# Turning the queries and keys of batches 1 to 3 with transposing transfers of 16-bit halves through DRAM in the place of TensorE

## Chip, cores and metric

One core of a Trainium2 chip runs the whole program. The metric is device time in microseconds (us), from one launch to its end; three runs of the kernel before gave a median of 1028.63 us (1025.24 to 1028.85). Lower is better.

## The reference, cut to what matters

Attention in which a query sees only the keys that chose the same one of 16 centroids, and then a feed-forward block with a squared ReLU:

```python
batch, n_heads, seq, head_dim = (4, 8, 768, 64)
n_clusters = 16
q_assign = np.argmax(np.einsum('bhsd,hcd->bhsc', q_n, c_n), axis=-1)
k_assign = np.argmax(np.einsum('bhsd,hcd->bhsc', k_n, c_n), axis=-1)
mask = q_assign[:, :, :, None] == k_assign[:, :, None, :]
scores = scale * np.matmul(q, k.transpose(0, 1, 3, 2))
scores = np.where(mask, scores, -1000000000.0)
attn = np.exp(scores - max); attn = attn / (sum + 1e-09)
attn_out = np.matmul(attn, v)
# (B, H, S, D) -> x of (3072, 512); w_in (512, 2048), w_out (2048, 512)
h = x @ w_in
out = (np.maximum(h, 0.0) ** 2) @ w_out
```

`q_n`, `k_n` and `c_n` are the rows divided by their norms. Queries, keys, values and centroids are float32; the weights come as 64-bit floats and are rounded in the kernel.

## The kernel before

**Pairs and units.** The 4 batches of 8 heads are worked on as 16 *pairs*: two heads of one batch, whose 64 features lie side by side on 128 partitions. Pairs 0 to 3 are batch 0, pairs 4 to 15 are batches 1 to 3. A pair has 768 queries in two halves of 384 and 768 keys in six chunks of 128. A *unit* is one half of the queries against two chunks of the keys, so a pair has six units. Batch 0 goes first with the first halves of all its pairs (units 0 to 11), then with the second halves (units 12 to 23); after that each pair of batches 1 to 3 takes six units in a row (24 to 95). The loop at L665 goes through the units, with two more rounds, since the product with v (`times_v`) of a unit comes two units after its scores.

**One unit of pairs 4 to 15.** `scores` (L368) issues eight matmuls into two PSUM tiles `sc`. ScalarE takes the exponentials in place (L395, two instructions), and VectorE multiplies by the mask (L399, four), by which the two PSUM tiles come free for the next unit: there are only two. GpSimd sums the exponentials (L409, L411). `times_v` adds eight matmuls. `finish` (L432), some units behind a half's end, sums on TensorE, takes the reciprocal on VectorE (L449) and sends a few rows to `seen` in DRAM (L455). Between these, `fill_steps` puts matmuls of the feed-forward block of batch 0 on TensorE (`ffn`, L469 and L482), in shares that are worked out ahead from a count of columns.

**Preparing the next pair.** For its scores a pair needs queries and keys with the features on the partitions: `qkT`, twelve blocks of 128x128 float32. They are loaded as rows (`load_qk`, four transfers of 192 KB on SP's queue; the pool `loads` has four buffers under the tag `qk`), and `turn` (L244) transposes them on TensorE, four blocks into one bank of PSUM, which ScalarE copies to SBUF (L253), three times for a pair. `logits` (L261) multiplies `qkT` by the centroids, `route` (L274) finds each row's centroid, and `spread` (L331) sends the choices through DRAM (`far`, L340) to all partitions (`qid`, L341), where L399 compares them. `prep` (L346) gives these steps as a list, which goes into `ahead` at the first unit of the pair before; each round of the loop takes up to three entries from `ahead` (L705 to L708), and an entry `None` is an empty turn. For pairs 5 to 15 the list is spaced out at L672, so that the three turns come in the first unit, `logits` in the second, `route` in the third and `spread` in the fourth.

**Order.** Each engine runs its instructions in the order that the framework's scheduler gave it, by the program's order and by priorities: the matmuls of `scores`, `times_v` and `logits` are pulled together (`together`, L86). So the place of an instruction can differ from that in the program, but it is fixed when the kernel is built. SP's queue too is worked through in order, and a transfer that waits holds up those behind it. `qkT` of pairs 0, 1 and 4 to 15 has two buffers (`qktp`).

**Behind the units.** After unit 95 the feed-forward block of the other batches runs in `ffn_pair`, with no part in the change. The weights are loaded and rounded during units 0 to 23 (`load_weights`, L137).

Of the kernel before, what the change touches and what calls it, by code (L numbers as in the profile page):

```python
# [8 lines left out]
F32 = mybir.dt.float32  # L9
BF16 = mybir.dt.bfloat16  # L10
I32 = mybir.dt.int32
U32 = mybir.dt.uint32
ALU = mybir.AluOpType
ACT = mybir.ActivationFunctionType
# [3 lines left out]
P = 128  # L18
# [6 lines left out]
def kernel(  # L25
# [10 lines left out]
    nc = tc.nc  # L36

    B, H, S, D = q.shape
    C = centroids.shape[1]
    NCH = S // P  # L40
# [4 lines left out]
    HP = H // 2  # L45
    NB = NCH // 2
    TB = NB * P
    NG = B * HP
# [10 lines left out]
    loads = ctx.enter_context(tc.tile_pool(name="loads", bufs=4))  # L59
    loads_v = ctx.enter_context(tc.tile_pool(name="loads_v", bufs=2))  # L60
    qktp = ctx.enter_context(tc.tile_pool(name="qktp", bufs=2))
# [12 lines left out]
    dram = ctx.enter_context(tc.tile_pool(name="dram", bufs=2, space=bass.MemoryType.DRAM))  # L74
# [21 lines left out]
    raw = {}  # L96
    raw_v = {}

    def load_qk(pair):
        if pair >= NG:  # L100
            return
        b, hp = divmod(pair, HP)
        raw[pair] = []
        for name, src in (("q_raw", q), ("k_raw", k)):
            t = loads.tile([P, NCH, 2 * D], F32, name=name, tag="qk")
            for e in range(2):
                (nc.scalar if pair == 0 and src is k else nc.sync).dma_start(
                    t[:, :, D * e : D * (e + 1)],
                    src[b, 2 * hp + e].rearrange("(p j) d -> p j d", p=P),
                )  # L110
            raw[pair].append(t)
# [15 lines left out]
    for fr in range(DFF // NW):  # L127
        for a in range(KT):
            cols = slice(fr * NW, (fr + 1) * NW)
# [9 lines left out]
    def round_weights(i):  # L139
# [22 lines left out]
        )  # L162
        dst, lo = dst.bitcast(I32), lo.bitcast(I32)
        nc.gpsimd.tensor_tensor(out=dst, in0=dst, in1=lo, op=ALU.add)
# [12 lines left out]
    nc.vector.memset(ups, UP)  # L177
    order_i = const.tile([P, C], I32, name="order_i")
    nc.gpsimd.iota(order_i, pattern=[[-1, C]], base=C, channel_multiplier=0)
# [60 lines left out]
    qkT = {}  # L240
# [3 lines left out]
    def turn(pair, part):  # L244
        if part == 0:
            pool = qkt_early if 2 <= pair < HP else qktp
            qkT[pair] = pool.tile([P, 2 * NCH, P], F32, name="qkT")
        pt = bank("pt", [P, 4, P])
        for i in range(4):
            which, c = divmod(4 * part + i, NCH)  # L250
            nc.tensor.transpose(out=pt[:, i], in_=raw[pair][which][:, c], identity=ident)  # L251
        dst = qkT[pair][:, 4 * part : 4 * part + 4]
        nc.scalar.copy(out=dst, in_=pt)  # L253
        if part == 2:
            raw.pop(pair)
            load_qk(pair + 2)

    lgs = {}
    last_logits = {}
# [1 line left out]
    def logits(pair):  # L261
        hp = pair % HP
        lg = (bank if pair else first_bank)("lg", [P, TB])
        last_logits[pair] = together(
            dict(
                out=lg[32 * g : 32 * g + 32], lhsT=cnT[:, 2 * C * hp : 2 * C * (hp + 1)],
                rhs=qkT[pair][:, NB * g : NB * (g + 1)], start=True, stop=True,
            )
            for g in range(4)
        )  # L270
        lgs[pair] = rbp.tile([P, TB], F32, name="lgs", tag="rb")
        nc.scalar.copy(out=lgs[pair], in_=lg)

    def route(pair):  # L274
        with tc.high_priority(offset=2000):
            number(pair)
# [34 lines left out]
    def turn_onehot(pair, which):  # L311
        if pair == 0:
            pt = first_bank("po", [P, NCH, P], BF16)
        else:
            pt = ps_f.tile([P, NCH, P], BF16, name="po", tag="f")
        for c in range(NCH):
            nc.tensor.transpose(
                out=pt[:, c],
                in_=oh[:, c % NB, 2 * which + c // NB].rearrange("p e c -> p (e c)"),
                identity=ident_b,  # L320
            )
        dst = qid[pair][1][:, which]
        src = pt.rearrange("p c n -> p (c n)")
        if which == 0 and pair == 0:
            nc.vector.tensor_copy(out=dst, in_=src)
        elif which == 0:
            nc.scalar.copy(out=dst, in_=src)
        else:
            nc.scalar.activation(out=dst, in_=src, func=ACT.Copy, bias=-BIG, scale=BIG)

    def spread(pair):  # L331

        src, dst = qid[pair]
        n = 4 * NB
        pb = ps_f.tile([n, P], BF16, name="pb", tag="f")
        nc.tensor.transpose(out=pb, in_=src.rearrange("p g e i -> p (g e i)"), identity=ident_b)
        row = once.tile([n, P], BF16, name="row", tag="b")
        nc.scalar.copy(out=row, in_=pb)  # L338
        far = dram.tile([n, P], BF16, name="far")
        nc.sync.dma_start(far, row)  # L340
        nc.sync.dma_start(  # L341
            dst.rearrange("p g e n -> p (g e n)"),
            far.rearrange("r n -> (r n)").partition_broadcast(P),
        )

    def prep(pair):  # L346
        return [
            lambda: turn(pair, 0), lambda: turn(pair, 1), lambda: turn(pair, 2),
            lambda: logits(pair), lambda: route(pair),
        ] + (  # L350
            [lambda i=i: turn_onehot(pair, i) for i in range(2)] if pair < HP
            else [lambda: spread(pair)]
        )

# [285 lines left out]
    def next_pair(u):  # L642

        pair, h, c = units[u]
        if c == 0 and pair + 1 < NG and h == 0 and (pair + 1) not in qkT:
            if pair + 1 < HP or pair >= HP:
                return pair + 1
        if c == 0 and h == 1 and pair == HP - 1:
            return pair + 1
        return None  # L650

    to_round = iter(range(len(weights)))
# [7 lines left out]
    ahead = []  # L660
# [4 lines left out]
    for u in range(len(units) + LAG + 1):  # L665
        if u < len(units):
            pair, h, c = units[u]
            if (p := next_pair(u)) is not None:
                ahead.extend(prep(p))
                if p > HP:  # L670

                    t0, t1, t2, lg, rt, *sp = ahead  # L672
                    ahead = [t0, t1, t2, lg, None, None, rt, None, None, *sp]
            if c == 0 and u + 3 < len(units) and units[u + 3][0] not in raw_v:
                load_v(units[u + 3][0])

            with behind_first(u):
                scores(pair, h, c)
        done = None
        if LAG <= u < len(units) + LAG:  # L680
            pair, h, c = units[u - LAG]
            times_v(pair, h, c)
            if c == NCH - 2:
                done = pair, h

        rounding += 4
        while rounding >= 3:
            rounding -= 3
            i = next(to_round, None)
            if i is not None:  # L690
                with tc.issue_after(last_exp[0]):
                    round_weights(i)
                if (i := next(loaded, None)) is not None:
                    load_weights(i)
            elif not later:
                early.close()
                for name, bufs in (("xT", 5), ("out", 2)):
                    later[name] = keep.enter_context(
                        tc.tile_pool(name=name + "_late", bufs=bufs, side="right",
                                     reuse_waits="tile")  # L700
                    )
        share = max(0, left[0] - RESERVE) * density(u) // max(1, sum(map(density, range(u, ENDS))))
        goal = left[0] - share
        fill_steps(share // 2)
        for _ in range(3):  # L705
            if ahead:
                with behind_first(u):
                    (ahead.pop(0) or int)()  # L708
        fill_steps(left[0] - goal)

        if not (done and first_half(*done)):
            ended.append(done)
            done = ended.pop(0)
        if done:
            pair, h = done
            with tc.high_priority(offset=1000) if pair < HP else ExitStack():
                finish(pair, h)
            b, hp = divmod(pair, HP)
            if h == 1:
                for d in (qkT, ids, qid):  # L720
                    d.pop(pair)
            if h == 1 or b == 0:
                raw_v.pop(pair)
            if hp == HP - 1 and (h == 1 or b == 0):
                for half in [(b, h)] if b == 0 else [(b, 0), (b, 1)]:
                    if half in PLAIN:
                        fill.append(ffn(*half))
# [3 lines left out]
    def check_sums():  # L731
# [20 lines left out]
    wtp, tp, sp, gp = (  # L752
        fast.enter_context(tc.tile_pool(name=name, bufs=1, reuse_waits="tile"))
        for name in ("wtp", "tp", "sp", "gp")
    )
# [207 lines left out]
```

## Time and profile before

| What | us |
|---|---|
| median of three runs | 1028.63 |
| lowest and highest | 1025.24 and 1028.85 |
| the profiled execution: its own time | 1025.6 |
| its span, first to last instruction | 1023.4 |
| VectorE busy in the span | 597.0 (58%) |
| ScalarE busy | 300.1 (29%) |
| GpSimd busy | 377.5 (37%) |
| first and last matmul of `scores`, from the span's start | 10.9 and 571.0 |
| first transposes of a pair of batches 1 to 3 | 145.2 |
| last such transposes | 521.5 |

The 1025.6 us of the profiled execution hold the span of 1023.4 us and 2.2 us around it. A line of the profile's groups gives the kernel's line, the engine, the operation, the tile written and the tiles read, the shapes and a count; behind the bar stand the busy time of the group, the mean duration of one instruction in ns, and the engine's idle time just before them with what ended it. PE is TensorE (PEld its weight loads, which run beside its matmuls), ACT is ScalarE, DVE is VectorE, POOL is GpSimd, SP is the engine that only issues transfers (SPq in the rows). In the timeline a row has the start, the time it covers, the engine, the line and a count, and in brackets the idle time before it. Matmuls overlap, so the mean of one is longer than the distance from one start to the next.

### The profile page before, as it was taken

The page shows a single profiled execution, that of the slowest core. Times are in us where ns is not written, and L with a number is a line of the kernel's source. Part 1 is how long each engine was busy: PE and PEld are TensorE (multiplying, and loading weights), DVE is VectorE, ACT ScalarE, POOL GpSimd, SP SyncE. Part 2 cuts the span into 40 slices and gives each one's busy share as a digit, 9 for nine tenths or more (in the row PEclk, how much of TensorE's full clock was granted, in tenths as well). Part 3 has the DMA queues.
Part 4 walks back from the last instruction along what each step waited for, and adds up shares of the span by engine and source line. Part 5 has one row for each costly group of instructions (what it writes and reads, how often), then busy time and mean ns, then how long its engine had stood idle before and what let it go on. Part 6 is the DMA issues. An engine that isn't in the chain of part 4 may idle for free.

```text
span 1023.4 us, 11682 instructions
## 1 busy us (share of the span) xinstructions
PE 1003.8 (98%) x4399; PEld 558.6 (55%) x4399; DVE 597.0 (58%) x907; ACT 300.1 (29%) x494; POOL 377.5 (37%) x277
## 2 busy tenths in 40 slices
PE   7999999999999999999999999999999999999997
PEld 3444444333334444443333455688755788656886
DVE  4679767665666566656686786722366523556421
ACT  5776564333333443443333111100011000111000
POOL 1337665445554645555556533000332001331000
PEclk9999999999999999999999999999999999999999
DMA  9664432021202102120100000000000000000000
GB/s 241 180 188 143 140 111 68 25 72 48 59 30 72 48 22 57 47 62 17 42 16 27 12 0 1 1 21 21 21 0 1 1 21 21 20 1 1 21 21 24
DMA packets 66239, 49.23 MB, mean 48 GB/s; under 512 B 52096, under 2 KB 57600, under 8 KB 66176
## 3 DMA queue, kind: packets, MB, share of 16 engines
q1 hardware_dynamic: 64464, 47.99, 16.2%
q8 instruction: 37, 0.61, 0.2%
q10 hardware_dynamic: 1712, 0.43, 0.2%
q14 instruction: 26, 0.21, 0.1%
HBM read 41.98 MB, written 6.33 MB: 47 GB/s over the span
## 4 chain that ended last, share of the span: by engine, by line
PE 93%; DVE 4%; DMA 1%; ACT 1%; issue 1%; SPq 0%; DVEq 0%; ACTq 0%
PE bank L592 21%; PE bank L561 21%; PE po L482 9%; PE ph L469 8%; PE av L89 7%; PE sc L89 7%; PE sc L92 7%; PE av L92 6%; PE pt L251 2%; PE sm L89 2%; PE sm L92 2%; DVE rb L449 1%; PE lg L89 1%; DVE ex L399 1%; DVE best L292 1%
## 5 line engine op out<-in xcount | busy, mean ns | idle before, releaser
L411 POOL TENSOR_TENSOR acc<-acc,ex 128x768 f32<-128x768 f32 x112 | 208.1, 1858 | 116.2 <-DVE ex L399 101.2
L399 DVE SCALAR_TENSOR_TENSOR ex<-qid,ids,sc 128x384 f32<-128x384 bf16 x288 | 158.1, 600 | 104.4 <-ACT sc L395 96.5
L92 PE MATMUL sc<-qkT 64*128 64x384 f32 x576 | 150.9, 502 | 1.9 <-DVE ex L399 1.6
L395 ACT ACTIVATE sc<-sc 128x768 f32<-128x768 f32 x144 | 108.4, 792 | 139.3 <-PE sc L92 139.2
L92 PE MATMUL av<-ex,v_raw 128*64 128x384 f32 x576 | 144.2, 494 | 0.0
L531 DVE TENSOR_TENSOR g<-bank,g 128x384 f32<-128x384 f32 x144 | 77.9, 556 | 80.6 <-PE bank L561 79.7
L550 POOL TENSOR_TENSOR w_s<-w_in 128x256 f32<-128x256 f32 x24 | 18.0, 752 | 276.8 <-PE bank L592 162.0
L482 PE MATMUL po<-w_out,gT 128*128 128x512 f32 x192 | 100.3, 626 | 0.0
L449 DVE RECIPROCAL rb<-sm 128x384 f32<-128x384 f32 x32 | 81.7, 2554 | 28.7 <-PE sm L92 28.6
L469 PE MATMUL ph<-xT,w_in 128*128 128x384 f32 x256 | 97.0, 506 | 0.0
L592 PE MATMUL bank<-w_out,g 128*128 128x256 f32 x432 | 95.2, 379 | 0.0
L592 PEld LDWEIGHTS bank<-w_out,g 128*128 128x128 f32 x432 | 82.1, 190 | 11.8
L89 PE MATMUL sc<-qkT 64*128 64x384 f32 x192 | 87.2, 534 | 0.2 <-DVE ex L399 0.2
L531 DVE TENSOR_TENSOR osb<-bank,osb 128x256 f32<-128x256 f32 x54 | 22.1, 423 | 107.6 <-PE bank L592 97.2
L409 POOL TENSOR_TENSOR acc<-ex 128x768 f32<-128x768 f32 x28 | 50.9, 1818 | 85.1 <-DVE ex L399 76.1
L89 PE MATMUL av<-ex,v_raw 128*64 128x384 f32 x192 | 82.2, 510 | 0.0
L92 PEld LDWEIGHTS sc<-qkT 64*128 64x128 f32 x576 | 65.0, 186 | 29.3 <-ACT row L338 2.8
L561 PE MATMUL bank<-xT,w_in 128*128 128x384 f32 x192 | 69.9, 487 | 0.0
L561 PE MATMUL bank<-x_t,w_s 128*128 128x384 f32 x192 | 69.8, 486 | 0.0
L561 PE MATMUL bank<-xT,w_s 128*128 128x384 f32 x192 | 69.8, 486 | 0.0
L469 PEld LDWEIGHTS ph<-xT,w_in 128*128 128x128 f32 x256 | 43.9, 189 | 46.0 <-issue 17.5
L592 PE MATMUL bank<-w_t,g 128*128 128x256 f32 x288 | 65.1, 379 | 0.0
(118 smaller groups left out, 1262.0 us busy)
## 6 DMA issues: line engine op xcount, KB each, us to landing
w_raw<-in_moe_w_in_dram SPq DMA_DIRECT2D x16, 512.0 KB
w_raw<-in_moe_w_out_dram SPq DMA_DIRECT2D x16, 512.0 KB
v_raw<-in_v_dram SPq DMA_DIRECT2D x20, 384.0 KB
q_raw<-in_q_dram SPq DMA_DIRECT2D x32, 192.0 KB
out_dram<-osb SPq DMA_DIRECT2D x23, 256.0 KB
k_raw<-in_k_dram SPq DMA_DIRECT2D x30, 192.0 KB
qid<-far SPq DMA_DIRECT2D x12, 384.0 KB
seen<-rb SPq DMA_DIRECT2D x32, 3.0 KB
```

Source lines behind the costliest of these rows:

```text
L89: last = nc.tensor.matmul(**next(products))
L92: last = nc.tensor.matmul(**product)
L395: last_exp[0] = nc.scalar.activation(out=t[:, 2 * i : 2 * i + 2] if pair < HP else src, in_=src, func=ACT.Exp, scale=SCALE).ins
L399: nc.vector.scalar_tensor_tensor(out=t[:, 2 * i + e], in0=qid[pair][1][:, h, e], scalar=ids[pair][:, ch % NB, 2 + ch // NB, e : e + 1], in ...
L409: nc.gpsimd.tensor_tensor(out=acc[pair, h], in0=t[:, 0:2], in1=t[:, 2:4], op=ALU.add)
L411: nc.gpsimd.tensor_tensor(out=acc[pair, h], in0=acc[pair, h], in1=t[:, 2 * i : 2 * i + 2], op=ALU.add)
L449: nc.vector.reciprocal(out=rb, in_=sm)
L469: nc.tensor.matmul(ph, lhsT=w_in[:, kk, f * P : (f + 1) * P], rhs=xT[b, h][:, kk], start=(kk == 0), stop=(kk == KT - 1),)
L482: nc.tensor.matmul(po, lhsT=gT[f][:, i * P : (i + 1) * P], rhs=w_out[:, f], start=(f == 0), stop=(f == FT - 1),)
L531: nc.vector.tensor_tensor(out=out, in0=bank, in1=to, op=ALU.add)
L561: nc.tensor.matmul(bank, lhsT=operands[j][0][:, kk], rhs=operands[j][1][:, kk], start=(kk == 0), stop=(kk == H2 - 1),)
L592: nc.tensor.matmul(bank, lhsT=operands[j][0][:, f], rhs=operands[j][1][:, f], start=(f == 0), stop=(f == F2 - 1),)
```

## The change

For pairs 4 to 15 the twelve transposes, their three PSUM banks and their three copies go. In their place `split_words` takes the loaded float32 words of a pair apart into two 16-bit halves: for q and for k, ScalarE copies twice, each 3 chunks x 2 halves x 128 features = 768 16-bit elements on each partition, from the words (every second half-word) to a tile `flat` in which all low halves of a row stand side by side and then all high halves. SP writes `flat` to DRAM (393 KB), as rows of 128 half-words; `words` holds 12 x 128 x 2 = 3072 such rows, 786 KB for a pair. `turn_words` then issues one transfer with `transpose=True`, which reads the 3072 rows of 128 half-words and writes 128 partitions of 3072 half-words: on partition d, for each row of q or k, the low and the high half of its feature d next to each other, and so the float32 word again. The tile is `qkT` as before.

The list of `prep` for these pairs is now: in the first unit `turn_words` of the next pair, nothing, and `split_words` of q of the pair after the next; in the second unit nothing; in the third `logits`, nothing, `split_words` of k; in the fourth `route`; in the fifth `spread`. The load of the following pair is issued behind the split of k. Pair 4 is split in units 12 and 15, outside the list, and its list starts at unit 18 (before: at 21). `flat` shares the four buffers of the loads, and the pool in DRAM has two of `words`.

```diff
+U16 = mybir.dt.uint16
...
         if part == 2:
             raw.pop(pair)
-            load_qk(pair + 2)
+            if pair in (0, 1, HP - 2):
+                load_qk(pair + 2)
...
+    words = {}
+
+    def split_words(pair, which):
+        if which == 0:
+            words[pair] = dram.tile([2 * NCH, P, 2, 2 * D], U16, name="words")
+        flat = loads.tile([P, NCH, 2, 2 * D], U16, name="flat", tag="qk")
+        src = raw[pair][which].bitcast(U16).rearrange("p c (d two) -> p c two d", two=2)
+        half = NCH // 2
+        for cols in (slice(0, half), slice(half, NCH)):
+            nc.scalar.copy(out=flat[:, cols], in_=src[:, cols])
+        nc.sync.dma_start(
+            words[pair][NCH * which : NCH * (which + 1)].rearrange("c p two d -> p c two d"),
+            flat,
+        )
+        if which == 1:
+            raw.pop(pair)
+            load_qk(pair + 1)
+
+    def turn_words(pair):
+        qkT[pair] = qktp.tile([P, 2 * NCH, P], F32, name="qkT")
+        nc.sync.dma_start(
+            qkT[pair].rearrange("p c n -> p (c n)").bitcast(U16),
+            words.pop(pair).rearrange("c p two d -> (c p two) d"), transpose=True,
+        )
...
     def prep(pair):
+        if pair < HP:
+            return [
+                lambda: turn(pair, 0), lambda: turn(pair, 1), lambda: turn(pair, 2),
+                lambda: logits(pair), lambda: route(pair),
+                lambda: turn_onehot(pair, 0), lambda: turn_onehot(pair, 1),
+            ]
+
+        split = [lambda i=i: split_words(pair + 1, i) for i in range(2 if pair + 1 < NG else 0)]
+        first, second = split or (None, None)
         return [
-            lambda: turn(pair, 0), lambda: turn(pair, 1), lambda: turn(pair, 2),
-            lambda: logits(pair), lambda: route(pair),
-        ] + (
-            [lambda i=i: turn_onehot(pair, i) for i in range(2)] if pair < HP
-            else [lambda: spread(pair)]
-        )
+            lambda: turn_words(pair), None, first, None, None, None,
+            lambda: logits(pair), None, second, lambda: route(pair), None, None,
+            lambda: spread(pair),
+        ]
...
-        if c == 0 and h == 1 and pair == HP - 1:
-            return pair + 1
+        if c == 0 and h == 1 and pair == HP - 2:
+            return HP
...
                 ahead.extend(prep(p))
-                if p > HP:
-
-                    t0, t1, t2, lg, rt, *sp = ahead
-                    ahead = [t0, t1, t2, lg, None, None, rt, None, None, *sp]
+            if u in (HP * NCH // 2, HP * NCH // 2 + 3):
+
+                split_words(HP, int(u > HP * NCH // 2))
```

## The prediction

> **What bounds the kernel now.** I read the page first: busy shares, the chain that ended last, the waits of TensorE.
>
> ```profile
> PE 1003.8 (98%) x4399; PEld 558.6 (55%) x4399; DVE 597.0 (58%) x907; ACT 300.1 (29%) x494; POOL 377.5 (37%) x277
> ...
> PE 93%; DVE 4%; DMA 1%; ACT 1%; issue 1%; SPq 0%; DVEq 0%; ACTq 0%
> ```
>
> TensorE is busy for 98% of the span and the chain runs over it for 93%, at a granted clock of 1.00 in every window. The longest wait of its matmuls is one of 6.4 us at the start, for the first q. So a matmul less is time gained, if nothing else then makes TensorE wait.
>
> Next the groups of the lines that go.
>
> ```profile
> L253 ACT COPY qkT<-pt 128x512 f32<-128x512 f32 x48 | 27.8, 591 | 37.3 <-PE pt L251 37.3
> L251 PE MATMUL pt<-ident,k_raw 128*128 128x128 f32 x96 | 16.7, 290 | 0.3 <-ACT qkT L253 0.3
> L251 PE MATMUL pt<-ident,q_raw 128*128 128x128 f32 x96 | 16.5, 290 | 7.3 <-DMA q_raw<-in_q_dram 6.4 <-DVE rb L449 0.9
> L150 ACT ACTIVATE w_raw<-w_raw 128x512 f32<-128x512 uint32 x32 | 22.0, 689 | 0.0
> ```
>
> Of 192 transposes 144 go (12 for each of 12 pairs). By busy time they are worth 144 x 33.2/192 = 24.9 us. That counts overlap with their neighbours, so I take the timeline, from one start to the start of what follows.
>
> ```profile
> 415.40 0.60 PE L251 MATMUL pt<-ident,q_raw 128*128 128x128 f32 x4
> 415.84 0.81 PE L469 MATMUL ph<-xT,w_in 128*128 128x384 f32 x2
> 416.58 0.59 PE L89 MATMUL sc<-qkT 64*128 64x384 f32 x1
> ...
> 418.07 0.44 PE L251 MATMUL pt<-ident,q_raw 128*128 128x128 f32 x2
> 418.35 0.38 PE L251 MATMUL pt<-ident,k_raw 128*128 128x128 f32 x2
> 418.66 0.54 PE L89 MATMUL av<-ex,v_raw 128*64 128x384 f32 x1
> ...
> 420.10 0.66 PE L251 MATMUL pt<-ident,k_raw 128*128 128x128 f32 x4
> 420.59 0.81 PE L469 MATMUL ph<-xT,w_in 128*128 128x384 f32 x2
> 421.33 0.59 PE L89 MATMUL sc<-qkT 64*128 64x384 f32 x1
> ...
> 423.67 0.51 PE L89 MATMUL lg<-qkT,cnT 128*32 128x384 f32 x1
> ```
>
> Here the three turns take 0.44 + 0.59 + 0.49 = 1.52 us of TensorE. Summed in this way over all twelve pairs I get 18.8 us, 1.57 a pair. The row of `lg` matters below.
>
> **The change, part by part.**
>
> *TensorE.* Minus 18.8 us (at most 24.9). The three PSUM banks a pair no longer taken from the feed-forward matmuls would add the 0.9 us of waits on L449 in the row above; I count nothing.
>
> *ScalarE.* It loses 36 copies of 0.585 us (median of L253), 21 us. It gains 48 copies of 768 elements. No copy of 16-bit halves from SBUF is in the trace. The nearest rows: 512 integers from SBUF to SBUF in 0.689 us (L150), and the slope between 384 elements in 0.480 (L272) and 768 in 0.792 (L395), 0.81 ns an element. That gives 0.69 + 256 x 0.00081 = 0.90 us, 43 us in all; from below 0.79. So ScalarE has 22 us more to do, 1.8 a pair. The cover: in a window of 50 us there (400 to 450) it is busy for 21.4. Without it, each copy stands before an exponential, whose result must pass the mask before the next scores find their PSUM free. What slack is there? In the unit that starts at 416.58 the four masks run from 418.49 to 420.68. The first scores of the next unit use the tile that the second mask frees, at 419.6, and the others, 0.75 us later, that of the fourth. They start at 421.33, so the slack is 1.4 us. The unit before (scores at 411.08, masks delayed by a 2.56 us reciprocal to 416.22, next scores at 416.58) has 1.1. Out of these go 0.59 + 0.49 = 1.08 us and 0.44 us of transposes, which leaves 0.3 and 0.7. ScalarE sits idle from 413.54 to 416.04 after the exponentials of the first of the two, so the copies mostly fit there; if one slips before an exponential, 0.90 - 0.3 = 0.6 us is lost. Bounds: nothing, and two such slips a pair, 12 x 1.2 = 14 us. I take 3 us, since the idle stretch holds both copies (1.8 of 2.5 us).
>
> *Transfers and SP's queue.* Each pair gains three: two writes of 393 KB and the transposing one of 786 KB. Each issue costs SP some 0.65 us (two q loads 1.30), 2 us a pair, on a queue that mostly waits. The loads of q and k stay four a pair, now behind the second split, about 16 us (three units) before the next first split; they need 6 us, as the next fence shows.
>
> ```profile
> 419.00:420.00 1.00, 1.00 (x8) 0.29 (x4) 1.00 (x3) 0.60 (x2) 0.00 (x0) 1.00 0.03 7
> 420.00:421.00 1.00, 1.00 (x8) 0.69 (x6) 0.68 (x2) 0.20 (x1) 0.17 (x1) 1.00 0.95 216
> 421.00:422.00 1.00, 1.00 (x6) 0.49 (x6) 0.00 (x0) 0.91 (x3) 1.00 (x1) 1.00 0.76 171
> 422.00:423.00 1.00, 1.00 (x7) 0.37 (x4) 0.00 (x0) 1.00 (x2) 0.92 (x2) 1.00 0.76 175
> 423.00:424.00 1.00, 1.00 (x6) 0.28 (x10) 0.71 (x2) 0.88 (x2) 1.00 (x1) 1.00 1.12 255
> ```
>
> The last two columns are the share of the DMA engines and GB/s. q and k of a pair were issued from 418.54 on, move from 420 and are through by about 424.2 (171 to 255 GB/s). The writes of `words` are of that size, behind them stand v, `far` and `qid`, and the transposing transfer reads them at the next first unit, some three units later: hidden. DMA engines were busy for 0.15 of the window 400 to 450, so there is room. `spread` moves from the fourth unit to the fifth. Its `qid` was issued at 401.36 for masks that run at 413.67; a unit of some 5 us later leaves 7 us for a transfer that took 3 (issued 436.37, quiet at 439.5). Hidden too.
>
> *The one wait that matters.* `logits` now waits for the transposing transfer, and TensorE, working in order, keeps all its matmuls behind it. The transfer waits for `words` (long landed) and for the buffer of `qkT` two pairs back (free after the last scores of that pair). In SP's queue it competes with `seen`, which waits for the reciprocal and went out at 413.78. So it starts at 411 to 414. `logits` ran at 423.67, in or after the second unit; one unit later (8.8 us from 421.33 to 430.09 there, 5 elsewhere) is about 428.7 to 432. Room: some 14 us from the later start, more from the earlier one.
>
> Does it land in 14 us? No transposing transfer is in the trace. From below: the plain loads of 786 KB in the same 3072 packets of 256 bytes, 1.5 us of lag and 4.2 of moving, 5.7 us. From above: 24 blocks of 128x128 half-words one after another, each with that lag of 1.5 us alone, 36 us; then TensorE waits 22 us a pair, 264 us in all. It is nearest to the first: the same bytes in the same rows, from DRAM to SBUF on the same queue. I take 6 to 13 us: no wait.
>
> The Trainium skill says two things here. "VectorE: DVE Perf Modes", section "The three transpose paths", gives 390 ns for a 128x128 bf16 transpose on TensorE and 1309 ns for one by the DMA crossbar, and its rules prefer TensorE where a PSUM result will do: this speaks against the change. "DMA: Bandwidth & Descriptors", section "Latency and other measured facts", has a measured 261 GB/s for transposing transfers. By the first, taken serially, 24 x 1.309 = 31.4 us a pair, 17.4 late, 209 us in all, and some 1219 us; by the second 3 us for 786 KB, and no wait. These are estimates from those pages; no run so far shows either.
>
> *Pair 4.* Its splits and transfer fall among the weight loads, where SP is held for 9 to 10 us at a time (L137 at 111.59 and 133.60), but three units of 6 to 7 us stand between the steps. At worst once some 10 us; I take 0.
>
> **Sum.** -18.8 + 3 = -16 us. On the profiled execution, 1025.6, that is 1010; the three runs of the kernel have a median of 1028.6, 3 us above it, so -16 gives 1012 for the median. A change under 0.5%, 5 us, can't be told from none here.
>
> **The rivals.**
>
> 1. *The transfer is late.* From 14 us on, each us costs 12 us. Against the 16 us gained, no gain is left at 15.4 us, and it is slower by more than 0.5% from 15.8. At 18 us: 1012 + 48 = 1060; at the upper bound of 36 us: 1012 + 264 = 1276. For: nothing in the trace shows such a transfer, and its elements of two bytes must come apart on 128 partitions. Against: the loads of the same bytes in 5.7 us. Chance 0.31.
>
> 2. *The freed time becomes a wait.* If the chain scores, exponential, mask, scores sets the unit's length, the 14 us of ScalarE's upper bound come back out of the 18.8, and the time is 1028.6 - 18.8 + 14 = 1024. For: slacks of only 0.3 and 0.7 us left in two units of six, DVE busy for 5.03 of 5.6 us in one. Against: the other four units have no transposes to lose, and the third, with 8.8 us, has several us of slack. Chance 0.09.
>
> 3. *The scheduler rearranges.* Without the banks of `turn` it may give `logits` or the feed-forward matmuls other places, and the waits on L449 (pb, 2.5 us in three cases) may move to `route`. A few us either way, 1026. Chance 0.02.
>
> **How the numbers follow.** The forecast has 0.58: 1012, within 1005 to 1020. Rivals 2 and 3 make the chance of the same, 0.11, rival 1 that of slower, 0.31. Low is 1003 (24.9 us gained in full, 1028.6 - 24.9 = 1003.7). High: rival 1 may take up to 0.2 of chance beyond the range; about 0.13 of it lies up to 18 us, so 1060.
>
> **What would show it.** Right: no L251 after batch 0 (the window 50 to 100 us); L92 with `lg` without DMA waits; the span shorter by 12 to 20 us; L253 with 12 rows; new copies of 0.8 to 0.9 us. Wrong: TensorE waiting for `words` at `lg`, some us twelve times (rival 1); more idle time on `sc` matmuls that L399 ends (rival 2).

## The result, and the profile after

The changed kernel takes 1044.84 us (median of four runs, 1042.97 to 1045.29) against 1028.68 us before: a ratio of 1.0162, 95% interval 1.0137 to 1.0186, slower by 1.6%. The forecast was 1012, faster. The profiled execution took 1045.11 us, with a span of 1043.2.

From the page of the changed kernel: busy shares, the granted clock in 40 slices, and the chain that ended last.

```profile
PE 1000.2 (96%) x4255; PEld 546.6 (52%) x4255; DVE 596.0 (57%) x907; ACT 313.9 (30%) x506; POOL 373.5 (36%) x277
...
PEclk9998998999999999999999999999999999999999
...
PE 75%; issue 7%; DVE 5%; DMA 4%; ACT 4%; POOL 3%; SPq 1%; POOLq 0%; ACTq 0%; DVEq 0%
PE bank L629 21%; PE bank L598 21%; PE po L519 9%; PE sc L90 5%; PE av L90 5%; PE sc L93 4%; PE av L93 4%; PE ph L506 4%; DMA q_raw<-in_q_dram 3%; PE sm L90 2%; POOL w_in L165 2%; DVE rb L486 1%; ACT flat L272 1%; DVE ex L436 1%; POOL acc L448 1%
```

TensorE has 144 instructions less, but its busy time fell by 3.6 us only, and the chain no longer runs over it alone: 25% now lies elsewhere, part of it on transfers of q and the new copies to `flat`. To see where, I compared the start of the scores, unit by unit, in the two timelines (us; the lines of the new kernel are up to 37 further down):

| first scores of unit | before | after | difference |
|---|---|---|---|
| 6 | 48.1 | 51.5 | +3.4 |
| 12 | 79.9 | 86.5 | +6.6 |
| 18 | 116.8 | 139.0 | +22.2 |
| 24 (pair 4) | 164.2 | 197.0 | +32.8 |
| 48 | 304.1 | 331.3 | +27.2 |
| 72 | 445.1 | 469.4 | +24.3 |
| 95, the last | 569.9 | 589.6 | +19.7 |

From unit 24 on, where the transposes are gone, the change gains 13.1 us. All of the loss, 32.8 us, falls into batch 0, which still turns its queries and keys on TensorE. Some 3 us of it are gone by unit 1 (first scores at 22.0 against 18.6 us), and they seem to belong to this execution, not to the change: six scores of unit 0 take 2.93 us in place of 1.55, and the profile's record of the clock, at 1.00, begins at 19.3 us in place of 10.4. The kernel with the transfer twice, further down, runs nothing ahead and has the same late start (21.8 us). The busy time by stretches of 50 us says the same. The first four rows are the kernel before, the next four the changed one, from 50 to 250 us (stretch and its length; PE, PEld, DVE, ACT and POOL; granted clock, DMA share, GB/s; the DMA share adds up the times of single packets and can pass 1):

```profile
50.00:100.00 50.00, 50.00 (x294) 22.91 (x294) 40.69 (x47) 35.24 (x56) 25.93 (x17) 1.00 0.54 166
100.00:150.00 50.00, 49.97 (x228) 23.81 (x228) 35.67 (x33) 28.89 (x49) 33.69 (x21) 1.00 0.39 127
150.00:200.00 50.00, 46.66 (x216) 19.46 (x215) 34.28 (x46) 23.31 (x40) 25.88 (x15) 1.00 0.23 59
200.00:250.00 50.00, 50.00 (x229) 20.08 (x231) 30.24 (x48) 17.17 (x27) 27.00 (x15) 1.00 0.23 61
```

```profile
50.00:100.00 50.00, 41.07 (x263) 18.01 (x261) 30.35 (x43) 37.37 (x57) 16.32 (x12) 0.98 0.87 240
100.00:150.00 50.00, 43.88 (x186) 19.83 (x183) 31.15 (x26) 29.62 (x49) 29.63 (x18) 0.95 0.83 213
150.00:200.00 50.00, 42.27 (x171) 17.99 (x169) 28.02 (x28) 35.51 (x60) 24.55 (x15) 0.90 0.73 192
200.00:250.00 50.00, 47.68 (x206) 17.72 (x206) 31.95 (x49) 21.43 (x32) 27.45 (x16) 1.00 0.34 87
```

TensorE idles for some 23 us of the first three stretches, the DMA engines are twice as busy, and the granted clock falls to 0.90. What TensorE waits for is ScalarE: its waits for ScalarE's results sum to 23.5 us (0.6 before), led by these (us in total, times, longest):

```profile
PE sc L90 <- ACT ex L432: 6.4, 2, 6.2
PE ph L506 <- ACT lgs L302: 4.0, 1, 4.0
```

Why are transfers there at all that belong to batches 1 to 3? The instructions on the new tiles answer that (duration min/median/max in ns, then the first and last start in us):

```profile
L272 ACT COPY flat<-q_raw x24: 810/830/862, 56.8 to 207.9; 128x768 uint16<-128x768 uint16 x24
L272 ACT COPY flat<-k_raw x24: 806/827/868, 58.4 to 210.2; 128x768 uint16<-128x768 uint16 x24
L273 SPq DMA_DIRECT2D words<-flat x24: 378/395/583, 58.8 to 211.0; - x24
L283 SPq DMA_TRANSPOSE qkT<-words x12: 2832/3642/5007, 106.7 to 530.0; - x12
```

The transposing transfers are spread up to 530 us, as the program asks. But all 48 copies and all 24 writes, for pairs up to 15, were issued between 57 and 211 us. The program asks for the last of them near unit 80, some 270 us later. Nothing held them. Before the change, a load for pair p+2 had to wait until pair p was turned, and the turn for one of two buffers of `qkT`. The new chain of load, copy and write ends in DRAM, and its SBUF buffers come free as soon as the write has left. The two places that the pool names for `words` did not hold it either: by 211 us the words of all twelve pairs were written and only two pairs' had been read (the third transposing transfer starts at 229.3). So the scheduler could issue the chain far ahead of its place, and did. The loads of q show it too, before and after:

```profile
L107 SPq DMA_DIRECT2D q_raw<-in_q_dram x32: 545/634/1645, 0.7 to 451.4; - x32
L108 SPq DMA_DIRECT2D q_raw<-in_q_dram x32: 545/570/808, 0.7 to 203.2; - x32
```

What this does shows around 93 us, in the timeline of the changed kernel:

```profile
90.03 0.67 ACT L149 ACTIVATE w_out<-w_raw 128x512 f32<-128x512 f32 x1
...
90.59 0.66 ACT L151 ACTIVATE w_raw<-w_raw 128x512 f32<-128x512 uint32 x1
...
91.14 0.49 PE L93 MATMUL sc<-ohT 64*128 64x384 bf16 x4
...
91.27 0.40 SPq L273 DMA_DIRECT2D words<-flat  x1
...
91.94 1.13 PE L93 MATMUL av<-ex,v_raw 128*64 128x384 f32 x5
...
92.58 0.56 SPq L108 DMA_DIRECT2D q_raw<-in_q_dram  x1
...
96.94 1.56 ACT L272 COPY flat<-q_raw 128x768 uint16<-128x768 uint16 x2 [5.69 <-issue]
98.41 1.50 ACT L432 ACTIVATE ex<-sc 128x768 f32<-128x768 f32 x2
...
99.27 1.00 PE L90 MATMUL sc<-qkT 64*128 64x384 f32 x1 [6.20 <-ACT ex L432]
```

SP issued one half of a q at 92.58, behind a write of `words`, and ScalarE's next instruction was the copy of that q. It stood from 91.25 to 96.94; the profile calls this "issue", but the copy began when the load had had its some 4 us. The exponentials of the current unit, whose scores had been ready since 91.6, came after it at 98.41, and TensorE had no free PSUM for the next scores until 99.27. The waits by releaser name the rest (us in total, times, longest):

```profile
ACT flat L272 <- DMA q_raw<-in_q_dram: 28.5, 8, 6.4
ACT flat L272 <- issue: 7.0, 2, 5.7
ACT flat L272 <- DMA k_raw<-in_k_dram: 2.1, 3, 1.5
```

So ScalarE stood for up to 37.6 us before copies; all but 1.7 us of it before copies whose words were read 147 to 324 us later.

### The profile page after: what moved, and what is told of

It reads as the page before. It is cut to its first block, busy times and chain, and to the rows that moved or that the text cites. A ratio compares the mean times of both kernels' runs of the same rounds, so it can differ in the third digit from the quotient of the medians.

```text
span 1043.2 us, 11500 instructions
## 1 busy us (share of the span) xinstructions
PE 1000.2 (96%) x4255; PEld 546.6 (52%) x4255; DVE 596.0 (57%) x907; ACT 313.9 (30%) x506; POOL 373.5 (36%) x277
## 4 chain that ended last, share of the span: by engine, by line
PE 75%; issue 7%; DVE 5%; DMA 4%; ACT 4%; POOL 3%; SPq 1%; POOLq 0%; ACTq 0%; DVEq 0%
PE bank L629 21%; PE bank L598 21%; PE po L519 9%; PE sc L90 5%; PE av L90 5%; PE sc L93 4%; PE av L93 4%; PE ph L506 4%; DMA q_raw<-in_q_dram 3%; PE sm L90 2%; POOL w_in L165 2%; DVE rb L486 1%; ACT flat L272 1%; DVE ex L436 1%; POOL acc L448 1%
## 5 line engine op out<-in xcount | busy, mean ns | idle before, releaser
L448 POOL TENSOR_TENSOR acc<-acc,ex 128x768 f32<-128x768 f32 x112 | 203.7, 1818 | 122.2 <-DVE ex L436 82.7
L93 PE MATMUL sc<-qkT 64*128 64x384 f32 x576 | 155.9, 516 | 1.2 <-DVE ex L436 0.8
L587 POOL TENSOR_TENSOR w_s<-w_in 128x256 f32<-128x256 f32 x24 | 18.0, 750 | 276.9 <-PE bank L629 162.0
L506 PE MATMUL ph<-xT,w_in 128*128 128x384 f32 x256 | 99.6, 519 | 7.4 <-ACT lgs L302 4.0
L90 PE MATMUL sc<-qkT 64*128 64x384 f32 x192 | 89.4, 547 | 8.8 <-ACT ex L432 6.4
```

Source lines behind the costliest of these rows:

```text
L90: last = nc.tensor.matmul(**next(products))
L93: last = nc.tensor.matmul(**product)
L448: nc.gpsimd.tensor_tensor(out=acc[pair, h], in0=acc[pair, h], in1=t[:, 2 * i : 2 * i + 2], op=ALU.add)
L506: nc.tensor.matmul(ph, lhsT=w_in[:, kk, f * P : (f + 1) * P], rhs=xT[b, h][:, kk], start=(kk == 0), stop=(kk == KT - 1),)
```

## The experiments

All eight kernels were compared with the kernel before on the same chip.

### Holding the copies in their place

```diff
         for cols in (slice(0, half), slice(half, NCH)):
-            nc.scalar.copy(out=flat[:, cols], in_=src[:, cols])
+            with tc.issue_after(last_exp[0]):
+                nc.scalar.copy(out=flat[:, cols], in_=src[:, cols])
```

`issue_after` sets only the order on ScalarE: the copy stands behind the last exponentials asked for before it. It adds no wait.

> The changed kernel with one edit: each copy of a split is queued on ScalarE behind the exponentials of the unit in which the program asks for it, so that splits can't be issued ahead of their place. Nothing else differs. Theory A (the splits and the loads behind them ran ahead into batch 0, ScalarE stood still for loads that had not landed, and TensorE behind it): the 33 us lost by the start of unit 24 come back and the gain of the later units stays, about 1012 us (1005 to 1020), granted clock 1.00. Theory B (the transposing transfers and the writes cost by themselves, by contention or by holding SP's queue): still 1035 to 1045. Theory C (the 43 us of copies on ScalarE cost, wherever they stand): between, 1022 to 1032.

Measured: 1009.03 us (1008.88 to 1010.26), ratio 0.9821, interval 0.9805 to 0.9837. One edit of order turned 1.6% slower into 1.8% faster, and into the best kernel of this study. Copies and writes in its trace now run through the batches, and ScalarE has no wait for a load before them:

```profile
L273 ACT COPY flat<-q_raw x24: 809/833/844, 78.5 to 467.2; 128x768 uint16<-128x768 uint16 x24
L274 SPq DMA_DIRECT2D words<-flat x24: 373/391/427, 82.5 to 477.8; - x24
```

The stretches of the held kernel, as above:

```profile
50.00:100.00 50.00, 50.00 (x296) 22.95 (x293) 40.52 (x46) 38.10 (x60) 26.10 (x17) 1.00 0.53 162
100.00:150.00 50.00, 50.00 (x225) 22.80 (x224) 38.60 (x38) 30.25 (x51) 33.69 (x21) 1.00 0.69 187
150.00:200.00 50.00, 47.98 (x201) 18.88 (x199) 32.99 (x42) 24.27 (x39) 26.85 (x16) 0.97 0.38 92
200.00:250.00 50.00, 50.00 (x222) 18.30 (x220) 32.67 (x48) 21.25 (x31) 29.56 (x17) 1.00 0.45 111
```

Unit 24 starts at 162.8 (1.4 us ahead of before), and the last at 553.6 (16.3 ahead). Theory A holds; B falls, since the transfers are the same ones, and C too.

### The traffic of the run-ahead without its copies

```diff
+            if 3 <= u < 24:
+                with tc.issue_after(last_load[0]):
+                    ...
+                    copy = dram.tile([P, NCH, 2 * D], F32, name="copy")
+                    for e in range(2):
+                        nc.sync.dma_start(
+                            copy[:, :, D * e : D * (e + 1)],
+                            side[b2, 2 * hp2 + e].rearrange("(p j) d -> p j d", p=P),
+                        )
+                    dump.append(copy)
+                    if len(dump) > 1:
+                        spare = dram.tile([NCH, P, 2 * D], F32, name="spare")
+                        nc.sync.dma_start(spare.rearrange("c p d -> p c d"), dump.pop(0))
```

(added to the held kernel; `last_load` is the last transfer of weights)

> The held kernel with the transfers of the run-ahead put back without their copies: in each of units 3 to 23 SP also moves one side of a pair of queries or keys (two transfers of 192 KB, from DRAM to DRAM in 256-byte pieces) and copies it once more in DRAM (384 KB); nothing reads them. Theory A with ScalarE's waiting as the cause: little is lost, 1012 to 1022, as no engine waits for these transfers. If the DMA engines' load and the late weights are the cause instead: 1030 to 1045, most of the 33 us lost again by unit 24.

Measured: 1014.54 us (1010.76 to 1019.07), ratio 0.9858, interval 0.9834 to 0.9883. Unit 24 starts at 169.1, 6.3 us behind the held kernel, in the slowest of the four runs (1019.07). The DMA engines are busier than in the changed kernel, and TensorE loses a fraction of what it lost there:

```profile
50.00:100.00 50.00, 50.00 (x311) 22.68 (x307) 37.70 (x48) 35.06 (x54) 24.18 (x17) 1.00 1.03 277
100.00:150.00 50.00, 46.77 (x208) 21.71 (x208) 35.34 (x31) 34.16 (x58) 34.06 (x22) 1.00 1.07 287
```

Of the 6.3 us, 2.9 are there by unit 1: this execution too has the late start. The rest is one wait of TensorE, for the transposing transfer of pair 4, which SP issued at 136.10 (at 108.71 in the held kernel):

```profile
PE lg L90 <- DMA qkT<-words: 3.2, 1, 3.2
```

ScalarE waits 8.0 us for `w_raw` of w_out as well. So traffic alone explains at most 6 of the 34.2 us between the changed and the held kernel at unit 24, and 3 if the late start is left out of both. The added transfers stand behind the weight loads in SP's queue, though; what the run-ahead costs where it stands before them is not shown by this kernel.

### Only pair 4 split

```diff
-        split = [lambda i=i: split_words(pair + 1, i) for i in range(2 if pair + 1 < NG else 0)]
-        first, second = split or (None, None)
+        first, second = None, None
...
-            words.pop(pair).rearrange("c p two d -> (c p two) d"), transpose=True,
+            words[HP].rearrange("c p two d -> (c p two) d"), transpose=True,
```

> The held kernel in which only pair 4 is loaded and split, and all twelve transposing transfers read its words: it leaves out 44 of the 48 copies, 22 of the 24 writes and the loads of q and k of pairs 5 to 15, so the output of these pairs is that of pair 4's queries and keys. Theory A: the copies cost 3 us or less, so 1009 to 1012. Theory C: 10 us or more below the held kernel.

Measured: 1011.58 us (1011.43 to 1013.14), ratio 0.9847, interval 0.9830 to 0.9863. Without 44 of 48 copies it is not faster than the held kernel; it is 2.6 us slower. Its profile has 2.9 us more of idle time and half clock (explained in the section on the prediction), mainly from a stop of 1.9 us at 324 us and the clock after it. So the copies cost nothing that shows where they stand, and neither do their loads and writes.

### A weaker hold

```diff
-            with tc.issue_after(last_exp[0]):
+            with tc.issue_after(gate[0] or last_exp[0]):
...
+            if u == HP * NCH - 1:
+                gate[0] = last_exp[0]
```

> The held kernel with a weaker hold: the copies for pairs 6 to 15 stand only behind the exponentials of unit 23, so they may run ahead as far as they like once batch 0 is through; those of pairs 4 and 5 stand as in the held kernel. Theory A, if it is the collision with the weight loads of batch 0 that makes the loads late: close to the held kernel, 1010 to 1020. If running ahead is harmful anywhere, because ScalarE stands in order behind each load: 1022 to 1040, with the loss now in units 24 to 45.

Measured: 1019.17 us (1018.22 to 1021.19), ratio 0.9918, interval 0.9901 to 0.9934. The time lies at the upper end of the first expectation, but the loss is where the second one puts it. The standstill of TensorE is back, behind batch 0 this time (stretch from 200 to 250 us, as above), and under it the same waits (us in total, times, longest):

```profile
200.00:250.00 50.00, 43.66 (x186) 16.09 (x184) 28.84 (x43) 27.94 (x39) 23.44 (x13) 1.00 0.90 209
```

```profile
ACT flat L274 <- DMA q_raw<-in_q_dram: 17.5, 8, 5.2
ACT flat L274 <- DMA k_raw<-in_k_dram: 4.5, 4, 1.8
```

Up to unit 24 it goes with the held kernel (162.0 against 162.8); between units 30 and 42 it loses 8.8 us against it. So running ahead still costs 10 us behind batch 0, where no weights are loaded: ScalarE stands for the late loads of the chain itself.

### The transfer twice

```diff
+        src = words.pop(pair).rearrange("c p two d -> (c p two) d")
+        for _ in range(2):
             nc.sync.dma_start(
-                qkT[pair].rearrange("p c n -> p (c n)").bitcast(U16),
-                words.pop(pair).rearrange("c p two d -> (c p two) d"), transpose=True,
+                qkT[pair].rearrange("p c n -> p (c n)").bitcast(U16), src, transpose=True
             )
```

> The held kernel with each transposing transfer issued twice, the second behind the first's landing into the same tile; so the queries and keys land some 5 us later (4.6 to 6.8 us is what one takes in the traces so far) and SP is held some 5 us longer. The rooms from issue to logits in the held kernel's trace are 17 to 20 us for pairs 6 to 15. Theory A (the transfer lands long before it is needed): 1008 to 1013, no wait of the logits on it. Rival 1 of the prediction (each us late costs 12 us): 1030 or more.

Measured: 1010.28 us (1009.86 to 1011.87), ratio 0.9825, interval 0.9789 to 0.9861: no different from the held kernel, and no wait of the logits on it. The transfer has at least its own length to spare.

### Logits a unit sooner

```diff
-            lambda: turn_words(pair), None, first, None, None, None,
-            lambda: logits(pair), None, second, lambda: route(pair), None, None,
-            lambda: spread(pair),
+            lambda: turn_words(pair), None, first, lambda: logits(pair), None, None,
+            lambda: route(pair), None, second, lambda: spread(pair),
```

> The held kernel with logits, route and spread back in the second, third and fourth unit, as before the change, so that the transfer has one unit (some 5 us) less: a room of some 12 us. Theory A: 1007 to 1013, the wider spacing of the change is neither needed nor harmful. If the landing is near its limit: slower than 1015, with waits of the logits on the transfer.

Measured: 1012.00 us (1011.26 to 1012.76), ratio 0.9835, interval 0.9799 to 0.9870. No wait on the transfer here either. It is some 3 us behind the held kernel, and all of that is there by unit 24 (166.3 against 162.8 us): TensorE waits once, 2.8 us, until VectorE has worked off the logits of pair 4, and has half clock after it. From there on the two keep the same distance, though `pb` waits 2.7 us in all for the reciprocal, which it doesn't in the held kernel. So batches 1 to 3 need the wider spacing neither for the transfer's sake nor otherwise.

### GpSimd in ScalarE's place, not held and held

```diff
-            nc.scalar.copy(out=flat[:, cols], in_=src[:, cols])
+            nc.gpsimd.tensor_copy(out=flat[:, cols], in_=src[:, cols])
```

> The changed kernel, not held, with its 48 copies on GpSimd in ScalarE's place: the loads and splits still run ahead into batch 0, but it is GpSimd that stands for late loads. ScalarE's part of theory A: no wait of ScalarE on loads of q, and the loss shrinks, 1012 to 1035, what stays being GpSimd's sums and weights that come late, and the traffic (5 us in the run with the transfers alone). If what costs is the traffic and the lateness of the weights, whoever copies: 1038 to 1050.

Measured: 1044.15 us (1042.03 to 1047.79), ratio 1.0158, interval 1.0113 to 1.0202. The loss is as large as with ScalarE: what I expected of theory A (1012 to 1035) missed, and the time lies in the other range (1038 to 1050). In its waits GpSimd now stands for the loads, ScalarE for weights that come late, and once the masks for a `qid` that stood in SP's queue:

```profile
ACT w_out L149 <- DMA w_raw<-in_moe_w_out_dram: 25.7, 14, 4.8
POOL flat L272 <- DMA q_raw<-in_q_dram: 25.7, 8, 7.1
...
DVE ex L436 <- DMA qid<-far: 16.2, 1, 16.2
PE sc L90 <- DVE ex L436: 15.4, 1, 15.4
```

The loss has another shape, though. Unit 24 starts at 181.3, 17.1 us behind the kernel before (32.8 with ScalarE); the wait for that `qid`, a stop of TensorE of 15.4 us at 186 with the clock at 0.50 behind it, adds most of the rest. Was GpSimd the wrong engine, or the running ahead? The next kernel holds its copies by the same means (`issue_after` behind GpSimd's last sum or rounded weight).

> The copies on GpSimd as in the run before, but held as in the held kernel: each stands on GpSimd behind the last sum or rounded weight that the program asked for before it. The run before lost as much as the change with GpSimd in ScalarE's place. If it is the running ahead that costs, whichever engine has the copies: 1007 to 1014, as the held kernel with ScalarE. If GpSimd is the wrong engine for the copies, because its sums then come late: 1020 to 1045.

Measured: 1009.99 us (1007.51 to 1012.06), ratio 0.9809, interval 0.9769 to 0.9849. Held, GpSimd does as well as ScalarE. So the engine that copies decides how the standstill reaches TensorE; that the chain runs ahead decides that it does.

## Why the prediction was wrong, point by point

A sum over the traces helps. Between the first and the last matmul, I added up the time in which no matmul was under way, and the time at a granted clock of 0.5. Half of the latter counts as lost, which is an estimate: TensorE may not be the limit all that time. The last column is the span less idle time and half.

```
                  span     idle   at 0.5   idle + half   rest
before          1023.4      7.6      0.0           7.6  1015.8
changed         1043.2     30.9     20.5          41.1  1002.1
held            1007.0      7.2      3.4           8.9   998.1
```

**The failing step** is the sentence on the loads and the writes: "The loads of q and k stay four a pair, now behind the second split, about 16 us (three units) before the next first split". It took the program's place for the place of issue, and the sum has no term for batch 0 but that of pair 4, at 0. The working checked that each wait had enough room, and never asked what keeps the new chain from being issued early. The removed `turn` had been that hold, through its two buffers of `qkT`: that is read from the kernel and from the loads in the trace before, and no run puts it back. Rival 3, a rearranging scheduler, had 0.02 and a few us, for logits and feed-forward matmuls only. In its place the runs showed 33.5 us more of idle time and half clock than before (41.1 - 7.6), and the hold alone brings 32.2 of them back. With it the time, 1009.03, lies in the predicted range. Rival 1 had the right sign, with the wrong transfer: not the transposing one was late, but loads that it did not need yet.

**TensorE's term**, -18.8 us: right. With the hold the rest falls by 17.7 us (1015.8 - 998.1), and the medians differ by 18.9 (1027.95 against 1009.03). In the changed kernel 13.7 of it were there already; 3 of the 4.0 us between are its late start. That 18.9 meets 18.8 so closely is luck: the spans of the two profiled executions differ by 16.4 us, as 1.3 us of idle time and half clock came in.

**The copies**, +3 us with 0.90 us each: 0.83 us each, and nothing that shows on the path in the held kernel. Rival 2 falls: idle time is 7.2 us there against 7.6.

**The transposing transfer**, 6 to 13 us against a room of 14: 4.6 to 6.8 us from issue to the last packet in the held kernel, and rooms of 17 to 20 us for pairs 6 to 15. Five stretches of 1 us after one issue at 229.30 in the changed kernel, with DMA share and GB/s last:

```profile
230.00:231.00 1.00, 1.00 (x7) 0.34 (x4) 1.00 (x3) 0.17 (x1) 0.92 (x2) 1.00 0.72 224
231.00:232.00 1.00, 1.00 (x3) 0.38 (x2) 0.76 (x2) 0.00 (x0) 1.00 (x1) 1.00 1.25 246
232.00:233.00 1.00, 1.00 (x6) 0.20 (x4) 0.00 (x0) 0.00 (x0) 0.92 (x2) 1.00 1.24 283
233.00:234.00 1.00, 1.00 (x8) 0.49 (x6) 0.53 (x1) 0.00 (x0) 0.95 (x1) 1.00 1.12 255
234.00:235.00 1.00, 1.00 (x8) 0.35 (x6) 1.00 (x1) 0.64 (x1) 0.98 (x1) 1.00 0.01 1
```

It moves its 786 KB in 3.4 us (the first row holds a transfer of `qid` besides), a little faster than the plain loads of the same bytes, 4.2 us; the nearest row was a good one. Of the two statements of the Trainium skill that the prediction weighed, the measured 261 GB/s in "DMA: Bandwidth & Descriptors", section "Latency and other measured facts", is near what this transfer reaches, 229 GB/s. The 1309 ns a block in "VectorE: DVE Perf Modes", section "The three transpose paths", can't be added up: 24 blocks took 5 us, not 31.

**SP's issue**, 0.65 us for each transfer: a transposing one holds SP for 2.8 to 5.0 us, six times as long. Twice that, in the kernel with two, cost nothing that shows.

**Pair 4**, 0: SP was not held for 9 to 10 us by single transfers; each of the two rows read there merges three issues of 0.33 us with the waits between them. In the held kernel nothing is lost at pair 4. Under added traffic its transfer came 3.2 us late.

What stays open: in the changed kernel TensorE stands for ScalarE, but not how much of ScalarE's own standing, in the 28 us beyond the traffic, comes from SP's queue, whose writes wait for the copies while loads and weights stand behind them. The unheld kernel with GpSimd shows that late weights and a late `qid` can stop TensorE too; no run parts the two.

## What to carry to other kernels

When a change takes an engine out of a chain, ask which buffer or order had held that chain back, and whether the new form still has such a hold; here the chain that ends in DRAM had none. Work that is issued early isn't free because its engine looks idle: ScalarE works in order, and one early copy of data that hadn't landed stopped everything behind it, for up to 6.4 us. So check the first and last start of each new group of instructions before its busy time: here 57 to 211 us, where the program asked for it up to 270 us later, pointed to the cause. And a forecast that is right in each price may still have the wrong sign if it takes the order of the program for the order of issue.

## What the hardware showed that I had not expected

Short stops of TensorE cost more than their length. Three stretches of the changed kernel around the stop shown above (stretch; PE, PEld, DVE, ACT, POOL; granted clock, DMA):

```profile
93.10:97.80 4.70, 0.00 (x0) 0.00 (x0) 1.31 (x3) 0.86 (x2) 1.28 (x1) 1.00 1.18 300
97.80:104.60 6.80, 5.33 (x18) 2.26 (x20) 4.07 (x3) 6.71 (x11) 3.69 (x2) 0.50 0.73 214
104.60:111.00 6.40, 6.40 (x29) 3.09 (x25) 6.37 (x6) 2.76 (x6) 6.13 (x4) 1.00 0.63 156
```

After 6.2 us without a matmul the clock is 0.50 for 6.8 us, and the first matmul of the scores takes 1.00 us in place of 0.59. All such stretches between the first and the last matmul lasted 3.4 us or a multiple, and in each execution their starts and ends lie on one grid of 3.413 us. I laid windows of 3.413 us on the half-clock stretches of the eight kernels that have some and summed TensorE's idle time in each window. In all 14 windows at full clock with 1.91 us of it or more, the next one ran at half clock; in none below 1.6 us did it; from 1.63 to 1.87 us it went both ways. So in the changed kernel a stop of 3.1 us (133.6 to 136.7) went free, as a window's edge parts it and the two windows have 1.86 and 1.33 us of idle time, while one of 1.9 us in a single window of the held kernel (168.0) cost another 1.7 us, by the same estimate. "TensorE: Matmul & The Clock Gate" of the Trainium skill, section "What's actually happening", describes a free-running window of 3413 ns, which these stretches fit; its advice to avoid gaps over some 3 us, in "Why this matters for your kernels", is too wide for this kernel, where 1.9 us in one window were enough.
